# Agent attention and a rational feed-forward layer on one core: every second product with v written to the upper half of the partitions

## The chip, the cores and the metric

The kernel runs on one core of a Trainium2 chip. The metric is device microseconds of one execution. Each time comes from repeated executions; a profile is one further execution with the hardware profiler on. TensorE multiplies matrices into PSUM, VectorE, ScalarE and GpSimd work elementwise, and SyncE (SP) issues the transfers.

## The reference

Two batches of 12480 tokens with 128 channels go through attention over 49 "agents" and then through a feed-forward layer with a rational activation of 2048 hidden units:

```
def sm(a, b):
    s = scale * (a @ b.transpose(0, 2, 1))
    s = s - s.max(-1, keepdims=True)
    e = np.exp(s)
    return e / (e.sum(-1, keepdims=True) + 1e-09)
a2k = sm(agents, k)              # 49 x 12480 for each batch
agent_v = a2k @ v                # 49 x 128
q2a = sm(q, agents)              # 12480 x 49
attn_out = q2a @ agent_v
h = x @ w_in                     # x: attn_out as (24960, 128)
P = a[0] + a[1] * h + a[2] * h2 + a[3] * h3
Q = 1.0 + np.abs(b[0]) * np.abs(h) + np.abs(b[1]) * h2
return (P / (Q + 1e-06)) @ w_out
```

The change is in `a2k @ v`: the sum over 12480 keys (padded to 98 chunks of 128) of a 49 x 128 product. A column of ones beside v gives the sum of the exponentials with it, so a product has 129 columns.

## The kernel before

**Two stages.** The first stage (up to about 66 us) does all of the attention of batch 0: scores of agents and keys (`sc_wide`, L209), their maxima (`mx_pe1`, `mx_pe2`, L227 and L235, which VectorE reads in L230 and L238), the exponentials (`ex_sub` L243, `ex_exp` L247) and the products with v (`pv_pe`, L253). Beside them the weights, which come in as 64-bit words, are decoded to float32 (`decode`: ScalarE L171 and L172, VectorE L175 to L178, GpSimd L181 and L182, VectorE L185). The second stage is the main loop (`main`) over 278 units of three chunks each: `mm1` (L439, L440) makes hidden values in one of two PSUM slots, ScalarE (L501, L515, L517), VectorE (L522, L530, L535) and GpSimd (L568, L573) the rational function, and `mm2` (L447) multiplies by w_out some units later. Every engine executes its instructions in the order in which the program issues them.

**Products of batch 0.** The 98 chunks are ten groups of 10 (`G0`); the last has 8. A chunk's exponentials, 128 keys by 49 agents, are the stationary operand, its part of v the moving one. Groups 0 to 4 add up in PSUM bank 4, groups 5 to 9 in bank 5, since the two have different maxima. After group 5 (`HG`) VectorE takes bank 4 times the factor `fac` (L783), at the end it adds bank 5 (L786), and `av_norm` (L263 to L265), the transpose (`avt_pe`, L268, to L271 and L272) and four matmuls with w_in (`m_pe`, L275) follow, which the main loop needs. Decoding of weight blocks stands between the groups in VectorE's order (`DECS`: behind groups 1, 3, 5 and 7). The queries' first scores (L374) stand behind group 2, their transposes (L401) behind group 7. At the end four products of the identity with itself (L789) run on TensorE.

**Products of batch 1.** They are 25 groups of up to 4 chunks (`G1`) in `a2k_stream`, of which the main loop takes one step per unit, when the PSUM bank that the output doesn't use is free: TensorE's part of the step runs behind `mm2`, the evictions one unit later (`pv_ev`, L257 for the first, L259 for others). Each group is a sum of its own in PSUM; VectorE adds them up in `av_acc`. `q_stream` takes steps beside it with the same bank.

Of the kernel before, what the change touches and what calls it, by code (L numbers as in the profile page):

```python
# [11 lines left out]
F32 = mybir.dt.float32  # L12
# [4 lines left out]
ALU = mybir.AluOpType  # L17
# [4 lines left out]
C = 128  # L22
A = 49
# [8 lines left out]
KR = 113  # L32
LO = 64
# [30 lines left out]
HG, MX1, MX2 = 5, 5, 0  # L64
# [16 lines left out]
def agent_attention_rational_moe(  # L81
# [12 lines left out]
    PE, ACT, DVE, POOL, SP = nc.tensor, nc.scalar, nc.vector, nc.gpsimd, nc.sync  # L94

    const = ctx.enter_context(tc.tile_pool(name="const", bufs=1))
# [5 lines left out]
    outs = [ps_p.tile([128, 512], F32, name=f"outb{i}") for i in range(2)]  # L102

    ident = const.tile([128, 128], F32, name="ident")
# [10 lines left out]
    S = const.tile([CK, NCK, A], F32, name="S")  # L115
    mx = const.tile([CK, 4, A], F32, name="mx")
    mb = const.tile([CK, 2, A], F32, name="mb")
    m49 = const.tile([A, 2], F32, name="m49")
    av_acc = const.tile([A, C + 1], F32, name="av_acc")
    avt = const.tile([128, KR], F32, name="avt")  # L120
    m_hi = [const.tile([128, DFF], F32R, name=f"m_hi{b}") for b in range(B)]
    m_lo = [const.tile([128, DFF], F32R, name=f"m_lo{b}") for b in range(B)]
# [6 lines left out]
    def ring(pool, n, shape, dt, nm):  # L129

        r = rings.setdefault((pool.name, nm), [[], 0])
        if len(r[0]) < n:
            r[0].append(pool.tile(shape, dt, name=f"{nm}_{len(r[0])}"))
        r[1] += 1
        return r[0][(r[1] - 1) % n]
# [4 lines left out]
    def load_k(pool, b, G, g, bufs):  # L140
        n = min(G, NCK - g * G) * CK
        t = ring(pool, bufs, [128, G * CK], F32, f"k{b}")
        o = b * NKP + g * G * CK
        for i in ((0, n // 2), (n // 2, n)) if (b, g) == (0, 0) else ((0, n),):
            SP.dma_start(out=t[:, i[0]:i[1]], in_=kT[:, o + i[0]:o + i[1]])
        k_t[b, g] = t

    def load_v(pool, b, G, g, bufs):
        n = min(G, NCK - g * G)
        t = ring(pool, bufs, [CK, G * (C + 1)], F32, f"v{b}")  # L150
        o = g * G * (C + 1)
        SP.dma_start(out=t[:, :n * (C + 1)], in_=vP[b, :, o:o + n * (C + 1)])
        v_t[b, g] = t.rearrange("p (c d) -> p c d", d=C + 1)
# [65 lines left out]
    def sc_pe(b, G, g, bank):  # L219
        kt = k_t.pop((b, g))  # L220
        for c in range(min(G, NCK - g * G)):
            PE.matmul(bank[:CK, c * A:(c + 1) * A], lhsT=kt[:, c * CK:(c + 1) * CK], rhs=ag[:, b * A:(b + 1) * A], start=True, stop=True)  # L222
# [3 lines left out]
    def mx_pe1(bank, src):  # L226
        PE.transpose(bank[:A, :CK], src, ident[:CK, :CK])  # L227

    def mx_ev1(bank, k=0):
        DVE.tensor_reduce(out=m49[:, k:k + 1], in_=bank[:A, :CK], axis=AX.X, op=ALU.max)  # L230
        st["d"] = ring(sm_p, 1, [A, A], F32, "d49")
        DVE.tensor_scalar(out=st["d"], in0=ident[:A, :A], scalar1=m49[:, k:k + 1], scalar2=None, op0=ALU.mult)
# [13 lines left out]
        s = S[:, g * G:min(g * G + G, NCK), :]  # L246
        ACT.activation(out=s, in_=s, func=AF.Exp, scale=SCALE)  # L247

    def pv_pe(b, G, g, bank, first, last):
        vt = v_t.pop((b, g))  # L250
        n = min(G, NCK - g * G)
        for c in range(n):
            PE.matmul(bank[:A, :C + 1], lhsT=S[:, g * G + c, :], rhs=vt[:, c, :], start=first and c == 0, stop=last and c == n - 1)  # L253

    def pv_ev(first, bank):
        if first:
            DVE.tensor_copy(out=av_acc, in_=bank[:A, :C + 1])  # L257
        else:
            DVE.tensor_tensor(out=av_acc, in0=bank[:A, :C + 1], in1=av_acc, op=ALU.add)  # L259

    def av_norm(src):
        r = ring(sm_p, 1, [A, 1], F32, "avr")
        DVE.tensor_scalar(out=r, in0=src[:, C:C + 1], scalar1=EPS, scalar2=None, op0=ALU.add)  # L263
        DVE.reciprocal(out=r, in_=r)
        DVE.tensor_scalar(out=av_acc[:, :C], in0=src[:, :C], scalar1=r, scalar2=co["rho_s"][:A], op0=ALU.mult, op1=ALU.mult)  # L265
# [360 lines left out]
    def a2k_stream(kv, b, G):  # L626
        ng = -(-NCK // G)
        load_k(kv, b, G, 0, 2)
        load_k(kv, b, G, 1, 2)
        yield (None, None, [])  # L630
        yield (None, None, [])
        for g in range(ng):
            if 1 <= g < ng - 1:
                load_k(kv, b, G, g + 1, 2)
            if g >= ng - 2:
                load_v(kv, b, G, g + 2 - ng, 2)

            def cp(bk, g=g):
                n = min(G, NCK - g * G)
                ACT.copy(out=S[:, g * G:g * G + n, :], in_=bk[:CK, :n * A].rearrange("p (c a) -> p c a", a=A))  # L640

            yield (None, lambda bk: sc_pe(b, G, g, bk), [("ACT", cp), ("DVE", lambda bk, g=g: group_max(G, g, bk))])
        row = 3 * ((ng - 2) // 2 % 2 == 0)
        yield (None, lambda bk: mx_pe1(bk, mx[:, row, :]), [("DVE", lambda bk: mx_ev1(bk))])
        yield (None, lambda bk: mx_pe2(bk), [("DVE", lambda bk: mx_ev2(bk))])
        for g in range(-2, ng):
            evs = []
            if g + 2 < ng:
                evs.append(("POOL", lambda bk, g=g: ex_sub(G, g + 2, POOL)))
            if 0 <= g + 1 < ng:  # L650
                evs.append(("ACT", lambda bk, g=g: ex_exp(G, g + 1)))
            if g < 0:
                yield (None, None, evs)
                continue
            if 1 <= g < ng - 1:
                load_v(kv, b, G, g + 1, 2)
            evs.append(("DVE", lambda bk, g=g: pv_ev(g == 0, bk)))
            yield (None, lambda bk: pv_pe(b, G, g, bk, True, True), evs)
        yield (None, None, [("DVE", lambda bk: av_norm(av_acc))])
        yield (None, avt_pe, [("DVE", avt_ev)])  # L660
        for pc in range(4):
            yield (None, lambda bk: m_pe(pc, bk), [("ACT", lambda bk: m_rnd(b, pc, bk)), ("DVE", lambda bk: m_rest(b, pc, bk))])

    with tc.manual_schedule():
        nc.scalar.preload_act_table_set("natural_log_exp_and_others")
        G = G0
        ng = -(-NCK // G)
        with tc.tile_pool(name="st", bufs=1) as sp, tc.tile_pool(name="pst", bufs=1, space=bass.MemoryType.PSUM) as pp:
            bank = [pp.tile([128, 512], F32, name=f"bank{i}") for i in range(6)]
# [23 lines left out]
            def load_next(g, most=99):  # L693

                while most > 0 and wanted and ready(*wanted[0], g):
                    kind, h = wanted.pop(0)
                    most -= 1
                    if kind == "v":
                        load_v(sp, 0, G, h, VB)
                    elif kind == "q":  # L700
                        load_q(h)
                    else:
                        raws[kind, h] = ring(sp, 4, [128, WP, 2], I32, "raw")
                        load_w(raws[kind, h], {"i": w_in, "o": w_out}[kind], h)
# [20 lines left out]
            for g in range(ng):  # L725
                bk = (bank[2 * (g % 3)], bank[2 * (g % 3) + 1])
# [26 lines left out]
                ex_sub(G, e, DVE)  # L753
                ex_exp(G, e)
            for g in range(ng):
                pv_pe(0, G, g, bank[4 if g < HG else 5], g in (0, HG), g in (HG - 1, ng - 1))
                if g == QPE:
                    q_pe(0, bank[0])
                    q_ev(0, bank[0])
                    q_exp(0)  # L760
                    q_sum(0)
                    for f in q_split(0):
                        f()
                if g == MX2:
                    mx_pe1(outs[0], mx[:, 1, :])
                    mx_ev1(outs[0], 1)
                if g == MX2 + 1:
                    mx_pe2(outs[1], 1)
                    mx_ev2(outs[1], 1)
                    for e in range(HG, ng):  # L770
                        ex_sub(G, e, DVE if e < HG + SUB_DVE else POOL, 1)
                        ex_exp(G, e)
                    fac = ring(sm_p, 1, [A, 1], F32, "fac")
                    DVE.tensor_tensor(out=fac, in0=m49[:, 0:1], in1=m49[:, 1:2], op=ALU.subtract)
                    ACT.activation(out=fac, in_=fac, func=AF.Exp, scale=SCALE)
                dec_at(g)
                if g == QTR:
                    q_tr(0, 0, bank[1])
                    q_tr(0, 1, bank[3])
                    q_trev(0, 0, bank[1], ACT.copy)  # L780
                    q_trev(0, 1, bank[3], ACT.copy)
                if g == HG:
                    DVE.tensor_scalar(out=av_acc, in0=bank[4][:A, :C + 1], scalar1=fac, scalar2=None, op0=ALU.mult)  # L783
                load_next(g)
            assert not wanted and not decs
            DVE.tensor_tensor(out=av_acc, in0=bank[5][:A, :C + 1], in1=av_acc, op=ALU.add)  # L786
            av_norm(av_acc)
            for _ in range(DUA):
                PE.matmul(outs[0][:, :128], lhsT=ident, rhs=ident, start=True, stop=True)  # L789
# [64 lines left out]
```

## Time and profile before

| | |
|---|---|
| median of 3 runs | 1321.06 us (1320.81 to 1327.85) |
| profiled execution | 1321.58 us |
| its span, first to last instruction | 1319.7 us |
| TensorE busy | 1255.2 us (95%) |
| VectorE busy | 1196.1 us (91%) |
| ScalarE busy | 1166.5 us (88%) |
| GpSimd busy | 1153.7 us (87%) |
| mean granted TensorE clock | 0.992 |

The busy shares are averages over both stages. In the rows below PE is TensorE's matmul, PEld its weight load, DVE VectorE, ACT ScalarE, POOL GpSimd, SPq the queue of SyncE. Matmuls overlap, and the end of one is modelled, so the start of one record against that of the next says more than its duration. [...]

### The profile page before, as it was taken

How to read it: one execution, taken by the hardware profiler on the slowest of the kernel's cores; microseconds unless marked ns; L12 is line 12 of the kernel's file. 1: busy time of each engine (PE TensorE's matmuls, PEld its weight loads, DVE VectorE, ACT ScalarE, POOL GpSimd, SP SyncE). 2: the span in 40 equal slices, each digit the busy share in tenths (PEclk: the TensorE clock that was granted, in tenths of full speed). 3: DMA queues.
4: the chain of work that ended last, by engine and by line, in shares of the span. 5: the costliest groups of instructions: out<-in, count | busy, mean ns of one | idle time of the engine just before them, and what ended most of it. 6: DMA issues, size and time to landing. Idle time of an engine off the chain costs nothing.

```text
span 1319.7 us, 13309 instructions
## 1 busy us (share of the span) xinstructions
PE 1255.2 (95%) x4815; PEld 786.3 (60%) x4815; DVE 1196.1 (91%) x984; ACT 1166.5 (88%) x736; POOL 1153.7 (87%) x562
## 2 busy tenths in 40 slices
PE   8979999998999999998999999999999999999998
PEld 8756666665566566665555555655655555565553
DVE  5888999989988888988999999999999999999996
ACT  3468999998889898997999999999999999999995
POOL 3448988988999998988899999999999999999991
PEclk9989999999999999999999999999999999999999
DMA  9411111111011111100000000000000000000000
GB/s 367 184 48 47 40 55 46 40 59 38 22 57 47 41 53 48 39 27 23 16 23 30 23 15 23 23 15 23 30 23 15 23 23 31 8 30 8 16 7 26
DMA packets 22971, 56.55 MB, mean 43 GB/s; under 512 B 2800, under 2 KB 9712, under 8 KB 22896
## 3 DMA queue, kind: packets, MB, share of 16 engines
q1 hardware_dynamic: 22896, 55.61, 12.7%
q8 instruction: 40, 0.66, 0.2%
q14 instruction: 35, 0.29, 0.1%
HBM read 42.82 MB, written 12.78 MB: 42 GB/s over the span
## 4 chain that ended last, share of the span: by engine, by line
PE 47%; DVE 23%; ACT 13%; POOL 9%; issue 6%; DMA 1%; SPq 0%; DVEq 0%; POOLq 0%; ACTq 0%
PE outb L447 25%; DVE u L522 8%; DVE w L530 8%; PE slot L439 8%; PE slot L440 7%; ACT x L501 6%; POOL u L568 5%; ACT w L517 3%; POOL u L573 3%; PE outb L374 3%; ACT w L515 2%; DVE u L535 2%; PE outb L253 2%; PE bank L209 1%; PE outb L222 1%
## 5 line engine op out<-in xcount | busy, mean ns | idle before, releaser
L447 PE MATMUL outb<-u,wo 128*128 128x480 f32 x1664 | 726.2, 571 | 36.6 <-DVE pT L406 21.4
L568 POOL TENSOR_TENSOR u<-u,w 128x1440 f32<-128x1440 f32 x204 | 668.6, 3290 | 0.0
L530 DVE SCALAR_TENSOR_TENSOR w<-slot,cf,x 128x1440 f32<-128x1440 f32 x278 | 474.9, 1708 | 89.8 <-ACT x L501 85.0
L447 PEld LDWEIGHTS outb<-u,wo 128*128 128x128 f32 x1664 | 309.5, 189 | 314.3 <-issue 230.5
L501 ACT ACTIVATE x<-slot,cf 128x1440 f32<-128x1440 f32 x278 | 405.5, 1459 | 96.7 <-PE slot L440 68.4
L522 DVE SCALAR_TENSOR_TENSOR u<-x,cf,slot 128x1440 f32<-128x1440 f32 x278 | 472.6, 1700 | 0.0
L573 POOL TENSOR_SCALAR u<-u,cf 128x1440 f32<-128x1440 f32 x204 | 387.8, 1902 | 93.7 <-DVE u L522 72.5
L439 PE MATMUL slot<-pT,m_hi 113*128 113x480 f32 x832 | 375.6, 452 | 10.9 <-DVE u L522 10.5
L515 ACT ACTIVATE w<-w,cf 128x2880 f32<-128x2880 f32 (+1 forms) x140 | 374.6, 2676 | 0.0
L517 ACT ACTIVATE w<-w 128x2880 f32<-128x2880 f32 (+1 forms) x140 | 361.8, 2585 | 0.0
L440 PE MATMUL slot<-pT,m_lo 113*128 113x480 f32 x832 | 317.4, 382 | 0.0
L439 PEld LDWEIGHTS slot<-pT,m_hi 113*128 113x128 f32 x832 | 157.6, 189 | 82.8 <-DVE u L522 40.9
L440 PEld LDWEIGHTS slot<-pT,m_lo 113*128 113x128 f32 x832 | 157.9, 190 | 40.8 <-issue 23.4
L535 DVE SCALAR_TENSOR_TENSOR u<-u,cf,w 128x1440 f32<-128x1440 f32 x74 | 134.0, 1816 | 0.0
L374 PEld LDWEIGHTS outb<-ag,q 128*120 128x120 f32 x400 | 45.6, 185 | 12.7 <-issue 8.2
L374 PE MATMUL outb<-ag,q 128*120 128x49 f32 x400 | 44.9, 265 | 0.9 <-DVE pT L406 0.7
L401 PEld LDWEIGHTS outb<-ident,p 120*113 120x113 f32 x200 | 27.5, 177 | 23.2 <-issue 20.0
L222 PEld LDWEIGHTS outb<-ag,k 128*128 128x128 f32 x196 | 26.4, 197 | 15.7 <-issue 8.8
L406 DVE CAST pT<-outb 113x480 fp32r<-113x480 f32 x50 | 32.4, 648 | 0.0
L454 ACT COPY o<-outb 128x480 f32<-128x480 f32 x42 | 23.0, 547 | 9.2 <-PE outb L447 9.2
L253 PEld LDWEIGHTS outb<-v,S 128*49 128x49 f32 x196 | 20.3, 123 | 17.6 <-issue 12.0
L401 PE MATMUL outb<-ident,p 120*113 120x120 f32 x200 | 29.2, 267 | 0.0
(132 smaller groups left out, 504.3 us busy)
## 6 DMA issues: line engine op xcount, KB each, us to landing
q<-qT SPq DMA_DIRECT2D x26, 480.0 KB, 3.4
outT<-o SPq DMA_DIRECT2D x52, 240.0 KB, 2.0
v<-vP SPq DMA_DIRECT2D x24, 258.0 KB, 2.7
k<-kT SPq DMA_DIRECT2D x24, 256.0 KB, 2.6
v<-vP SPq DMA_DIRECT2D x9, 645.0 KB, 11.1
k<-kT SPq DMA_DIRECT2D x8, 640.0 KB, 8.9
raw<-w_in SPq DMA_DIRECT2D x4, 512.0 KB, 10.8
raw<-w_out SPq DMA_DIRECT2D x2, 512.0 KB, 10.6
```

The source lines that it names most:

```text
L374: PE.matmul(bank[:CH, c * A:(c + 1) * A], lhsT=qt[:, c * CH:(c + 1) * CH], rhs=ag[:, b * A:(b + 1) * A], start=True, stop=True)
L439: PE.matmul(s[:, j, :BT], lhsT=m_hi[b][:KR, f], rhs=rhs, start=True, stop=False)
L440: PE.matmul(s[:, j, :BT], lhsT=m_lo[b][:KR, f], rhs=rhs, start=False, stop=True)
L447: PE.matmul(outs[blk % 2][:, :BT], lhsT=wo[:, fc, :], rhs=g[:, j, :], start=fc == 0, stop=fc == NFC - 1)
L501: ACT.activation(out=x, in_=h, func=AF.Square, bias=co["xb"])
L515: ACT.activation(out=r, in_=r, func=AF.Ln, bias=arm["lb"])
L517: ACT.activation(out=r, in_=r, func=AF.Exp, scale=-1.0)
L522: DVE.scalar_tensor_tensor(out=y, in0=x, scalar=co["kap"], in1=h, op0=ALU.add, op1=ALU.mult)
L530: DVE.scalar_tensor_tensor(out=w, in0=h, scalar=co["mu"], in1=x, op0=ALU.max, op1=ALU.add)
L535: DVE.scalar_tensor_tensor(out=view("u", u), in0=view("u", u), scalar=arm["om"], in1=view("w", u), op0=ALU.add, op1=ALU.mult)
L568: POOL.tensor_tensor(out=view("u", g), in0=view("u", g), in1=view("w", g), op=ALU.mult)
L573: POOL.tensor_scalar(out=y, in0=y, scalar1=1.0, scalar2=arm["om"], op0=ALU.mult, op1=ALU.add)
```

## The change

In both batches the even chunks of a group write PSUM partitions 0 to 48 and the odd ones 64 to 112 (`LO` = 64, `KR` = 113). The two halves must be added. [...] Batch 0 does this twice, once for bank 4 (the copy behind group 5, the matmul behind group 6) and once for bank 5; batch 1 adds up both halves at once over all groups (113 partitions instead of 49) and does it once at the end, in a step of its own.

```
+    av_two = const.tile([KR, C + 1], F32, name="av_two")
-    def pv_pe(b, G, g, bank, first, last):
+    def pv2_pe(b, G, g, bank, first=True, last=True):
         vt = v_t.pop((b, g))
         n = min(G, NCK - g * G)
         for c in range(n):
-            PE.matmul(bank[:A, :C + 1], lhsT=S[:, g * G + c, :], rhs=vt[:, c, :], start=first and c == 0, stop=last and c == n - 1)
+            o = c % 2 * LO
+            PE.matmul(bank[o:o + A, :C + 1], lhsT=S[:, g * G + c, :], rhs=vt[:, c, :], start=first and c < 2, stop=last and c >= n - 2)
-    def pv_ev(first, bank):
+    def pv2_ev(first, bank):
         if first:
-            DVE.tensor_copy(out=av_acc, in_=bank[:A, :C + 1])
+            DVE.tensor_copy(out=av_two, in_=bank[:KR, :C + 1])
         else:
-            DVE.tensor_tensor(out=av_acc, in0=bank[:A, :C + 1], in1=av_acc, op=ALU.add)
+            DVE.tensor_tensor(out=av_two, in0=bank[:KR, :C + 1], in1=av_two, op=ALU.add)
+    def pv2_sum(bank):
+        PE.matmul(bank[:A, :C + 1], lhsT=ident[LO:KR, LO:KR], rhs=av_two[LO:KR, :], start=True, stop=True)
+    def pv2_both(bank):
+        DVE.tensor_tensor(out=av_acc, in0=bank[:A, :C + 1], in1=av_two[:A, :], op=ALU.add)
+        av_norm(av_acc)
...
-        yield (None, None, [("DVE", lambda bk: av_norm(av_acc))])
+        yield (None, pv2_sum, [("DVE", pv2_both)])
...
-                pv_pe(0, G, g, bank[4 if g < HG else 5], g in (0, HG), g in (HG - 1, ng - 1))
+                pv2_pe(0, G, g, bank[4 if g < HG else 5], g in (0, HG), g in (HG - 1, ng - 1))
+                if g == HG + 1:
+                    pv2_sum(outs[0])
...
                 if g == HG:
+                    DVE.tensor_copy(out=av_two[LO:KR, :], in_=bank[4][LO:KR, :C + 1])
                     DVE.tensor_scalar(out=av_acc, in0=bank[4][:A, :C + 1], scalar1=fac, scalar2=None, op0=ALU.mult)
+                if g == HG + 1:
+                    DVE.scalar_tensor_tensor(out=av_acc, in0=outs[0][:A, :C + 1], scalar=fac, in1=av_acc, op0=ALU.mult, op1=ALU.add)
...
+            DVE.tensor_copy(out=av_two[LO:KR, :], in_=bank[5][LO:KR, :C + 1])
+            pv2_sum(outs[1])
             DVE.tensor_tensor(out=av_acc, in0=bank[5][:A, :C + 1], in1=av_acc, op=ALU.add)
+            DVE.tensor_tensor(out=av_acc, in0=outs[1][:A, :C + 1], in1=av_acc, op=ALU.add)
             av_norm(av_acc)
```

## Rows read from the trace of the kernel before

**Rows 1.** Busy time in stretches of the span; columns as in the first line.

```profile
core 0: us, PE busy (x) PEld busy (x) DVE busy (x) ACT busy (x) POOL busy (x), PEclk, DMA share, GB/s
30.00:58.00 28.00, 26.46 (x231) 25.12 (x229) 25.08 (x44) 11.93 (x23) 13.90 (x12) 1.00 0.58 224
...
355.00:590.00 235.00, 232.03 (x920) 144.22 (x920) 205.88 (x167) 212.81 (x139) 216.51 (x114) 1.00 0.16 46
700.00:1200.00 500.00, 476.78 (x1666) 286.45 (x1665) 472.23 (x336) 471.16 (x261) 477.50 (x210) 1.00 0.07 22
```

**Rows 2.** The same stretches, for ScalarE's first instruction of a unit (L501) alone.

```profile
355.00:590.00 235.00, 73.10 (x50) 1.00 0.16 46
700.00:1200.00 500.00, 171.12 (x117) 1.00 0.07 22
```

**Rows 3.** The chain of waits from 355 to 590 us, shares by line.

```profile
by line: PE outb L447 38.9%; PE slot L439 13.1%; PE slot L440 11.1%; PE outb L253 8.9%; DVE w L530 5.8%; DVE u L522 5.5%; ACT x L501 5.0%; PE outb L374 2.8%; issue 1.9%; DVE u L535 1.7%; ACT w L517 1.1%; ACT w L515 1.1%; PE outb L401 1.0%; 
```

**Rows 4.** Timeline of TensorE's matmuls around one group of batch 1; start, duration.

```profile
429.28 1.77 PE L447 MATMUL outb<-u,wo 128*128 128x480 f32 x4
430.98 1.09 PE L253 MATMUL outb<-v,S 128*49 128x129 f32 x8
432.00 0.49 PE L439 MATMUL slot<-pT,m_hi 113*128 113x480 f32 x1
```

**Rows 5.** Timeline of TensorE's matmuls in the first stage.

```profile
33.92 2.41 PE L253 MATMUL bank<-v,S 128*49 128x129 f32 x20
36.27 0.42 PE L235 MATMUL outb<-d,ones 49*128 49x49 f32 x2
...
38.96 1.88 PE L374 MATMUL bank<-ag,q 128*120 128x49 f32 x16
40.77 11.27 PE L253 MATMUL bank<-v,S 128*49 128x129 f32 x100
51.97 1.08 PE L401 MATMUL bank<-ident,p 120*113 120x120 f32 x8
52.98 4.19 PE L253 MATMUL bank<-v,S 128*49 128x129 f32 x36
```

**Rows 6.** Timeline of VectorE in the first stage, with its idle time before.

```profile
35.59 0.24 DVE L232 TENSOR_SCALAR d<-ident,m 49x49 f32<-49x49 f32 x1
36.73 0.21 DVE L238 COPY mb<-outb 128x49 f32<-128x49 f32 x1 [0.89 <-PE outb L235]
...
53.29 0.34 DVE L783 TENSOR_SCALAR av_acc<-bank,fac 49x129 f32<-49x129 f32 x1
...
57.91 0.28 DVE L786 TENSOR_TENSOR av_acc<-bank,av_acc 49x129 f32<-49x129 f32 x1
```

**Rows 7.** Timeline of TensorE's weight loads around the group of rows 4.

```profile
430.98 0.17 PEld L253 LDWEIGHTS outb<-v,S 128*49 128x49 f32 x2 [0.70 <-ACT x L501]
...
431.68 0.12 PEld L253 LDWEIGHTS outb<-v,S 128*49 128x49 f32 x1
...
432.00 0.19 PEld L439 LDWEIGHTS slot<-pT,m_hi 113*128 113x128 f32 x1 [0.19 <-issue]
...
433.20 0.41 PEld L447 LDWEIGHTS outb<-u,wo 128*128 128x128 f32 x2
```

**Rows 8.** The instructions of tile av_acc: duration least, median, most in ns.

```profile
L257 DVE COPY av_acc<-outb x1: 278/278/278, 357.7 to 357.7; 49x129 f32<-49x129 f32 x1
```

**Rows 9.** Busy time in the two stretches of half clock (PEclk 0.50).

```profile
60.80:64.20 3.40, 3.40 (x6) 1.27 (x5) 1.34 (x3) 1.37 (x2) 1.53 (x2) 0.50 0.42 113
...
91.50:98.30 6.80, 6.80 (x18) 4.99 (x19) 4.86 (x5) 2.87 (x4) 5.62 (x6) 0.50 0.14 39
```

**Rows 10.** Timeline from the last sum to the loop's first ScalarE instruction.

```profile
59.26 0.26 PE L268 MATMUL bank<-ident,av_acc 49*128 49x49 f32 x1 [1.00 <-DVE av_acc L265]
59.56 0.20 ACT L271 COPY avt<-bank 128x49 f32<-128x49 f32 x1 [3.98 <-PE bank L268]
60.15 3.09 PE L275 MATMUL outb<-wi,avt 128*113 128x512 f32 x4 [0.63 <-DVE avt L272]
...
66.90 1.47 ACT L501 ACTIVATE x<-slot,cf 128x1440 f32<-128x1440 f32 x1 [0.67 <-DMA k<-kT]
```

**Rows 11.** Waits of SP's own queue from 25 to 66 us: total, times, longest.

```profile
SPq L164 <- DVE wo L185: 16.5, 1, 16.5
```

More of the change, by code (lines that the diff above doesn't have):

```diff
@@ L656, in a2k_stream @@
                 load_v(kv, b, G, g + 1, 2)
-            evs.append(("DVE", lambda bk, g=g: pv_ev(g == 0, bk)))
-            yield (None, lambda bk: pv_pe(b, G, g, bk, True, True), evs)
-        yield (None, None, [("DVE", lambda bk: av_norm(av_acc))])
+            evs.append(("DVE", lambda bk, g=g: pv2_ev(g == 0, bk)))
+            yield (None, lambda bk: pv2_pe(b, G, g, bk), evs)
+        yield (None, pv2_sum, [("DVE", pv2_both)])
         yield (None, avt_pe, [("DVE", avt_ev)])
```

## The prediction

> **What bounds the kernel now.** I read the page first: its share of busy time (TensorE 95%, VectorE 91%, ScalarE 88%, GpSimd 87%) names no bound, because the kernel has two stages that both hold the changed products. So the second view is the table of stretches. In 30 to 58 us TensorE is busy 26.46 of 28.00 us and VectorE 25.08; in 355 to 590 us, where the products of batch 1 run inside the main loop, TensorE is busy 232.03 of 235.00 us and GpSimd 216.51; in 700 to 1200 us, without them, every engine lies near 95% [rows 1]. The reader is to see that only in the second stretch one engine stands out. The third view counts units of the loop by their first ScalarE instruction: 50 in 235 us are 4.70 us each, 117 in 500 us are 4.27 [rows 2]. So the loop is slower where batch 1 is worked on, and TensorE is why. The fourth view, the chain of waits of that stretch, says how much of it is L253: 8.9% of 235 us, 20.9 us [rows 3]. There are 25 groups of products in it (98 products, four to a group), each some 1.02 us from its first record to the next line's [rows 4], together some 25; so about 83% of what is taken from a group should come off the time.
>
> In the first stage I put the timeline of TensorE [rows 5] beside that of VectorE [rows 6]. TensorE ends its last product of batch 0 at about 57.1 us. VectorE comes to the last sum, L786, at 57.91 us, straight from decoding weights and not from a wait. So VectorE sets that end, with TensorE 0.8 us behind its back: a gain on TensorE alone is worth little here.
>
> **The products, part by part.** A product in float32 is two records: 196 records are 98 products. A run of 100 records takes 11.27 us with the last one's latency of 0.27 in it (20 records in 2.41 and 36 in 4.19 give 0.113 and 0.112), so one takes (11.27 - 0.27)/99 = 0.111 us [rows 5]. The change sends every second product to the other half of the partitions. If the two halves work at the same time, but records start in order and a product's second record follows its first on the same half, then the second record of one product runs with the first of the next. Eight records take five steps and not eight, twenty take eleven. Nothing in the trace has a matmul on partitions 64 and up alone, so it can't show this. The bounds are: no gain (eight steps), and three steps of 0.111 = 0.33 us a group.
>
> What the trace shows is near this. Entering and leaving a group costs a pause: L447 ends streaming at 429.28 + 4 x 0.40 = 430.88 us and the first load of L253 is at 430.98; the group ends streaming at about 431.90 and the load of L439 stands at 432.00, whereas the load of L447 at 433.20 is made while L440 still streams [rows 4, 7]. So a stationary block of 49 columns is already treated as another shape, and alternation between two such blocks doesn't add a shape. I take it that the halves overlap. [...]
>
> [...] First the row: the loads of L253 go on at the pace of the matmuls, the second 0.05 us behind the first (two are 0.17 us, one 0.12) [rows 7], and 0.111 a record leaves no room for an uncovered load. [...] The row stands for one half only, so the uncovered load is a rival below.
>
> **Main loop.** 24 groups x 0.33 and 0.11 of the last, short one are 8.1 us of TensorE; 83% of it is 6.7 us. The added sum with the identity is one group more: two records and two pauses, 0.22 + 0.20 = 0.4 us, paid on the same chain. VectorE's added instruction is priced by the copy, 0.28 us [rows 8]; VectorE is idle 29 us of this stretch, which hides it; without cover it costs its 0.28. The wider evictions (113 partitions for 49) read the same 129 elements each, so I price them at nothing: lower bound zero, upper bound doubled, 25 x 0.28 = 7 us of an engine with 29 us free. Sum: -6.3 us. Check against other engines: 235 - 6.3 = 228.7 us makes GpSimd 94.7% busy, VectorE 90.0%, ScalarE 93.1%, all under the 95.5%, 94.4% and 94.2% that they reach in 700 to 1200 us [rows 1]. So no other engine stops the gain.
>
> **First stage.** Here order matters. The sum of the upper half of bank 4 is issued on TensorE behind group 6 and needs VectorE's copy of that half, which stands just ahead of L783, behind the decoding of a weight block. Behind this sum on TensorE wait group 7, the transposes of q, groups 8 and 9.
>
> - VectorE gets a little earlier: mb (L238) waits 0.89 us for L235, which is queued behind group 1. With group 1 at eleven steps, it ends at 35.2 us; L232 is done at 35.83, L235 starts at about 35.9 and not 36.27, so 0.4 us are gained [rows 5, 6]. L783's place comes at 52.9, the copy there ends at 53.2.
> - TensorE gets far ahead: L235 until 36.2, group 2 until 37.5, q until 39.3, groups 3 to 6 (41 steps, 4.6 us) until 43.9. It then stands idle until 53.2 us: 9.3 us. Before, it reached this place at 40.77 + 80 x 0.111 = 49.6.
> - From 53.2 it still has: the sum 0.4, group 7 1.2, transposes with their pauses 1.0, a pause 0.1, groups 8 and 9 (19 steps) 2.1: 4.8 us at 2.4 GHz. But it comes out of a pause. The granted clock was at 0.50 (1.2 GHz) from 60.8 to 64.2 us, after a stretch with pauses of 1.0 and 0.6, and from 91.5 to 98.3 [rows 9, 10]. A pause of 9 us should bring it there too; one such stretch costs half its length, 1.7 to 3.4 us. I take 1.7, that of the nearest row. TensorE ends at 59.7, its result stands at 60.0 to 60.2.
> - VectorE's own work: copy 0.28, L783, a wait of some 0.3 for the sum, one instruction like L783 (0.34), and the decoding of 4.28 (53.63 to 57.91): it is there at 58.6, before TensorE. So TensorE is late next.
> - Tail: copy 0.28 (60.48), the sum by the pattern of L268 to L271 (0.30 and the issue: 60.85), with L786 under its cover, one more add 0.28: 61.1. L786 ended at 58.19. The stage loses 2.9 us; 1.2 if the clock stays at 2.4 GHz, 4.6 with the longer stretch.
>
> This delay isn't hidden later: av_acc, L268, the four L275 and the first slot follow each other up to the loop's first ScalarE instruction at 66.90 us [rows 10]. The queue of SP stood 16.5 us at its next load of weights, for VectorE's L185 [rows 11], which is shifted likewise, so these loads move along with their users.
>
> Sum: -6.3 + 2.9 = -3.4 us. The profiled execution took 1321.58 us (span 1319.7, 1.9 around it), 0.5 above the median of 1321.06: 1318.2 us.
>
> **Rivals.**
> 1. Loads uncovered (chance 0.20). At each change of half a load of about 0.043 us shows (0.17 less 0.12), then a product costs 0.111 + 0.043 = 0.154: a group saves 0.2 us. Main loop: 24 x 0.2 x 0.83 - 0.3 = -3.8; first stage 1.1 more for the 28 products left, +4.0. 1321.8 us.
> 2. No overlap at all (0.14), the other side: products go one after another as before. The wait for the copy then decides alone. TensorE is at the sum at 49.6, waits until 53.6, has 0.4 + 2.2 + 1.0 + 0.1 + 4.0 = 7.7 us left, and ends at 61.3, or 63.0 with a slow stretch; with the tail the stage loses 4.2 to 5.9 us, the loop another 0.3: 1326 to 1328 us. It decides as soon as a group of eight takes over 0.8 us.
> 3. A pause at each change of half (0.05): 0.10 us more, on rival 2, for each of 98 products in the loop (83% of 9.8 us) and of the 28 behind the first sum (2.8 us): 1327 + 8 + 3 = 1338. Against it speaks that both blocks have the same 49 columns.
> 4. Both slow stretches of the clock go (0.13). TensorE was busy all of the 3.4 and 6.8 us at half clock [rows 9]; at 2.4 GHz they give back up to 1.7 and 3.4 us. The denser work just ahead of L275 speaks for the first, nothing for the second but that it is moved: 1318.2 - 5.1 = 1313.1.
>
> **How the numbers follow.** My forecast has the rest, 0.48, with a range of its own of 1315.5 to 1321. No change that can be told is within 0.5%, 6.6 us: 1314.5 to 1327.7. Faster: rival 4, with a little of the forecast's edge, 0.14. Slower: rival 3 and the upper part of rival 2, 0.14. The range leaves out rival 3 and the edges of 2 and 4: 1313 to 1327.5.
>
> **What would show it.** Right: in the main loop a group of eight L253 records (now another line) takes 0.6 and not 1.0 us, and 355 to 590 us hold one to two units more; in the first stage TensorE idles 9 us ahead of the sum with a granted clock of 0.5 behind it, and the first ScalarE instruction of the loop comes at about 70 us. Wrong: groups of 0.9 us (rival 2), of 0.7 (rival 1), the loop's start at 67 us or earlier (the stall is hidden, or TensorE isn't that far ahead), or a loop that keeps 4.70 us a unit though its groups are shorter: then TensorE wasn't its bound.

## The result, and the profile after

In the first comparison the changed kernel took 1314.54 us in the median of 7 runs (1313.03 to 1318.83), the kernel before 1327.85 (7 runs, 1320.81 to 1330.11): ratio 0.9915, 95% interval 0.9888 to 0.9942 (the two medians alone would give 0.990, as that of the kernel before lies among its longer times). The forecast was 1318.2 us in a range of 1313.0 to 1327.5. The times of most kernels here lie in two groups 6 to 9 us apart, for a reason shown below (one instruction near the end); a second comparison, with 12 runs of the change, gave 0.9963 (0.9935 to 0.9990). So the change is faster, by 0.4% to 0.85% according to how many runs of each kernel fell into which group; both intervals lie below 1. The two profiled executions, 1321.58 and 1315.57 us, both belong to the shorter times (that instruction takes 3.06 us in each); their 6.0 us are taken apart here.

The starts of the units' first ScalarE instruction, read from the two timelines, say where the time went:

| | before | after | gained in the stretch |
|---|---|---|---|
| unit 0 (end of the first stage) | 66.90 | 70.42 | -3.52 |
| unit 60 | 344.02 | 346.94 | 0.60 |
| unit 112 (products of batch 1 over) | 585.97 | 583.39 | 5.50 |
| unit 130 | 670.81 | 664.89 | 3.34 |
| unit 277 (last) | 1295.30 | 1289.32 | 0.06 |

**A group of products.** The timeline of TensorE after, around one group of batch 1, which answers to [rows 4]:

```profile
420.50 2.58 PE L457 MATMUL outb<-u,wo 128*128 128x480 f32 x6
423.01 0.65 PE L256 MATMUL outb<-v,S 128*49 128x129 f32 x8
423.58 0.48 PE L449 MATMUL slot<-pT,m_hi 113*128 113x480 f32 x1
```

Cut to the start of the group, the same timeline shows loads and matmuls in pairs:

```profile
423.00 0.13 PEld L256 LDWEIGHTS outb<-v,S 128*49 128x49 f32 x2 [0.70 <-ACT x L511]
423.01 0.32 PE L256 MATMUL outb<-v,S 128*49 128x129 f32 x2
```

Eight records take 0.65 us with the last one's duration of 0.27 in it, where they took 1.09. The reader is to see that two records stand within 0.32 us: one of them alone takes 0.312 us, so the second starts about 0.01 us behind the first. The others follow in pairs too, at 423.15, 423.26 and 423.38 us: eight records are four pairs, four steps. From its first record to the next line a group takes 0.57 us and not 1.02: 0.44 us less, where 0.33 was forecast. The pauses on entering and leaving are near those of before, 0.09 and 0.08 us against 0.10: L457's last record starts at 422.51 and streams for 0.40, like those ahead of it, and the first load stands at 423.00; the last pair streams until 423.38 + 0.11 = 423.49, and L449 starts at 423.58.

**The stretch of the products**, unit 60 to unit 112, in the table of stretches; columns as in [rows 1]. Before:

```profile
344.02:585.97 241.95, 238.18 (x937) 147.23 (x936) 213.43 (x172) 219.51 (x145) 222.92 (x116) 1.00 0.15 46
```

After:

```profile
346.94:583.39 236.45, 228.06 (x937) 136.28 (x936) 214.63 (x172) 219.05 (x144) 223.45 (x117) 1.00 0.16 47
```

TensorE's busy time fell by 238.18 - 228.06 = 10.1 us, the stretch by 5.5: the rest turned into idle time of TensorE (3.8 us before, 8.4 after). The chain of waits after, in the same stretch, answers to [rows 3], which has it from 355 to 590 us of the kernel before:

```profile
by line: PE outb L457 22.1%; DVE u L532 11.1%; issue 9.9%; ACT x L511 9.4%; PE slot L449 8.6%; DVE w L540 8.2%; PE slot L450 7.4%; ACT w L525 5.3%; PE outb L384 3.6%; DVE u L545 3.3%; ACT w L527 3.3%; PE outb L256 2.8%; DVE pT L416 1.3%; DV
```

The share of L447 (now L457) falls from 38.9% to 22.1%, and that of all TensorE lines shown from 75.8% to 44.5%; VectorE's and ScalarE's lines take their place. GpSimd stands in neither row as shown.

**The first stage.** TensorE after, answering to [rows 5], and VectorE, answering to [rows 6]:

```profile
43.55 6.12 PE L256 MATMUL bank<-v,S 128*49 128x129 f32 x80
55.11 0.66 PE L265 MATMUL outb<-av_two,ident 49*49 49x129 f32 x2 [5.45 <-DVE av_two L795]
55.71 2.39 PE L256 MATMUL bank<-v,S 128*49 128x129 f32 x20
58.03 1.95 PE L411 MATMUL bank<-ident,p 120*113 120x120 f32 x8
59.91 2.38 PE L256 MATMUL bank<-v,S 128*49 128x129 f32 x36
62.69 0.42 PE L265 MATMUL outb<-av_two,ident 49*49 49x129 f32 x2 [0.40 <-DVE av_two L801]
```

```profile
54.76 0.30 DVE L795 COPY av_two<-bank 49x129 f32<-49x129 f32 x1
...
55.82 0.34 DVE L798 SCALAR_TENSOR_TENSOR av_acc<-outb,fac,av_acc 49x129 f32<-49x129 f32 x1 [0.38 <-PE outb L265]
...
58.88 0.68 DVE L186 SCALAR_TENSOR_TENSOR wo<-z,r 128x512 f32<-128x512 f32 x1
62.33 0.30 DVE L801 COPY av_two<-bank 49x129 f32<-49x129 f32 x1 [2.77 <-PE bank L256]
...
63.46 0.15 DVE L273 TENSOR_SCALAR avr<-av_acc 49x1 f32<-49x1 f32 x1
```

TensorE waits 5.45 us for the copy of bank 4's upper half to `av_two`, which the matmul with the identity reads, and then VectorE waits 2.77 us for TensorE. The granted clock, in the table of stretches after, answers to [rows 9]:

```profile
36.50:46.60 10.10, 9.48 (x70) 8.72 (x70) 8.51 (x21) 6.61 (x13) 3.08 (x3) 0.50 0.74 274
53.50:60.30 6.80, 5.19 (x34) 4.23 (x36) 5.52 (x11) 2.08 (x4) 4.79 (x3) 0.50 0.00 0
65.10:68.40 3.30, 3.29 (x7) 1.24 (x8) 1.77 (x3) 1.78 (x3) 0.69 (x1) 1.00 0.44 96
```

Twenty records take 2.39 us behind the pause of 5.45 us, at a granted clock of 0.50, and 1.31 at 1.00 (below). The third row is the four matmuls with w_in: at 1.00 now, while before they met the 0.50 of [rows 9]. The first row is a stretch that the kernel before doesn't have. It follows a pause that grew with the shorter products of group 0, before and after:

```profile
33.68 0.31 PE L227 MATMUL outb<-ident,mx 128*49 128x128 f32 x1 [1.54 <-DVE mx L191]
```

```profile
35.06 0.31 PE L228 MATMUL outb<-ident,mx 128*49 128x128 f32 x1 [2.65 <-DVE mx L192]
```

All seven profiles with the changed first stage have this pause of 2.65 us and a stretch at half clock that begins at 34.1 to 36.7 us; none of the seven with the first stage of before has one there.

And 1.37 us of the later start have nothing to do with the change: the first transfers of k landed later in this execution, as they did, by 1.1 and 0.5 us, in two profiles with the first stage of before (the loop's change and the step alone, below). TensorE's first run of scores in each, before and after:

```profile
8.62 11.41 PE L209 MATMUL bank<-ag,k 128*128 128x98 f32 x100 [0.73 <-DMA k<-kT]
```

```profile
9.99 11.41 PE L210 MATMUL bank<-ag,k 128*128 128x98 f32 x100 [2.15 <-DMA k<-kT]
```

From the copy's place (L783 before) to the normalisation (L263, now L273) it is 4.94 us before and 8.70 after, from there to the loop's first ScalarE instruction 8.67 and 6.96.

**The end of batch 1.** The 3.34 us between units 112 and 130 come from one place, unit 114 to 115: 9.44 us before, 5.54 after; the other units of the stretch give 0.56 of these 3.90 back. The timeline before, of GpSimd, VectorE and TensorE there:

```profile
590.82 3.30 POOL L568 TENSOR_TENSOR u<-u,w 128x1440 f32<-128x1440 f32 x1
591.72 2.48 DVE L265 TENSOR_SCALAR av_acc<-av_acc,avr,cf 49x128 f32<-49x128 f32 x1
...
599.00 0.64 DVE L406 CAST pT<-outb 113x480 fp32r<-113x480 f32 x1
599.70 1.60 PE L447 MATMUL outb<-u,wo 128*128 128x480 f32 x2 [3.65 <-DVE pT L406]
```

and after:

```profile
594.82 1.07 PE L457 MATMUL outb<-u,wo 128*128 128x480 f32 x2 [1.61 <-DVE pT L416]
...
602.67 0.90 DVE L275 TENSOR_SCALAR av_acc<-av_acc,avr,cf 49x128 f32<-49x128 f32 x1
```

Before, the last step of the normalisation runs beside a product of GpSimd, takes 2.48 us and ends 0.08 us behind it (594.20 and 594.12 us), and it stands ahead of the second transpose of q (L406), for which TensorE then waits 3.65 us, where the loop goes over to the next block of 480 queries. After, the step for the sum of the halves lies between, the normalisation comes three units later, and TensorE waits 1.61 us.

### The profile page after: what moved, and what is told of

It reads as the page before. It is cut to its first block, busy times and chain, and to the rows that moved or that the text cites. A ratio compares the mean times of both kernels' runs of the same rounds, so it can differ in the third digit from the quotient of the medians.

```text
span 1313.7 us, 13330 instructions
## 1 busy us (share of the span) xinstructions
PE 1238.9 (94%) x4821; PEld 768.8 (59%) x4821; DVE 1196.2 (91%) x989; ACT 1166.7 (89%) x736; POOL 1154.7 (88%) x562
## 4 chain that ended last, share of the span: by engine, by line
PE 43%; DVE 24%; ACT 15%; POOL 9%; issue 8%; DMA 1%; SPq 0%; DVEq 0%; POOLq 0%; ACTq 0%
PE outb L457 22%; DVE u L532 9%; DVE w L540 9%; ACT x L511 7%; PE slot L449 7%; PE slot L450 6%; POOL u L578 5%; ACT w L527 3%; ACT w L525 3%; POOL u L583 3%; PE outb L384 3%; DVE u L545 2%; PE bank L210 1%; PE outb L223 1%; DVE pT L416 1%
## 5 line engine op out<-in xcount | busy, mean ns | idle before, releaser
L457 PE MATMUL outb<-u,wo 128*128 128x480 f32 x1664 | 725.7, 570 | 36.6 <-DVE pT L416 19.7
L457 PEld LDWEIGHTS outb<-u,wo 128*128 128x128 f32 x1664 | 309.2, 189 | 314.0 <-issue 230.5
L449 PE MATMUL slot<-pT,m_hi 113*128 113x480 f32 x832 | 374.3, 450 | 11.0 <-DVE u L532 10.6
L449 PEld LDWEIGHTS slot<-pT,m_hi 113*128 113x128 f32 x832 | 157.0, 189 | 82.9 <-DVE u L532 41.0
L545 DVE SCALAR_TENSOR_TENSOR u<-u,cf,w 128x1440 f32<-128x1440 f32 x74 | 135.3, 1834 | 0.0
L223 PE MATMUL outb<-ag,k 128*128 128x49 f32 x196 | 25.4, 274 | 3.8 <-DVE mx L201 3.7
```

The lines of the kernel that those rows point to most:

```text
L449: PE.matmul(s[:, j, :BT], lhsT=m_hi[b][:KR, f], rhs=rhs, start=True, stop=False)
L457: PE.matmul(outs[blk % 2][:, :BT], lhsT=wo[:, fc, :], rhs=g[:, j, :], start=fc == 0, stop=fc == NFC - 1)
L545: DVE.scalar_tensor_tensor(out=view("u", u), in0=view("u", u), scalar=arm["om"], in1=view("w", u), op0=ALU.add, op1=ALU.mult)
```

## The experiments

**The loop's change alone**: the first stage is that of before.

```
-                pv2_pe(0, G, g, bank[4 if g < HG else 5], g in (0, HG), g in (HG - 1, ng - 1))
-                if g == HG + 1:
-                    pv2_sum(outs[0])
+                pv_pe(0, G, g, bank[4 if g < HG else 5], g in (0, HG), g in (HG - 1, ng - 1))
...
```

> Only batch 1 (the main loop) has the change; the first stage is that of before. Theory (the first stage loses 2.2 us to the wait on TensorE, the loop gains by itself): the loop's first ScalarE instruction at 66.9 us, or 1.4 later where a transfer of k lands late, then the same loop as with the whole change: about 2 us less than with it, some 9 us less than before. Rival (the first stage costs nothing, its later start is a late transfer alone): the same time as with the whole change, 6 us less than before.

1313.38 us against 1321.95 of before, ratio 0.9941 (0.9919 to 0.9964); unit 0 at 66.54 us though k came 1.1 us late. Units 60 to 112 take 236.37 us, as with the whole change. The theory holds: the loop gains by itself, and the first stage gives part of it back. (That unit 0 comes even earlier than expected is the clock at the four matmuls with w_in, at 1.00 in this profile: the first four records take 1.94 us there, and 3.09 before.)

**The first stage's change alone.**

```
-            evs.append(("DVE", lambda bk, g=g: pv2_ev(g == 0, bk)))
-            yield (None, lambda bk: pv2_pe(b, G, g, bk), evs)
-        yield (None, pv2_sum, [("DVE", pv2_both)])
+            evs.append(("DVE", lambda bk, g=g: pv_ev(g == 0, bk)))
+            yield (None, lambda bk: pv_pe(b, G, g, bk, True, True), evs)
+        yield (None, None, [("DVE", lambda bk: av_norm(av_acc))])
```

> Only batch 0 (the first stage) has the change; the loop is that of before. Theory: TensorE waits some 5 us ahead of the sum of bank 4, works at 1.2 GHz behind it and ends behind VectorE; the loop starts 2.2 us later than before for equal arrival of k, and the time is 2 us more than before. Rival (no cost): equal to before within 0.5 us.

1324.11 us against 1321.95, ratio 1.0012 (0.9988 to 1.0036): by the time alone no cost can be told. By the trace it can. From the copy's place to the normalisation it takes 9.30 us against 4.94, to unit 0 16.26 against 13.61. The theory holds by the trace, with a cost above the 2.2 us that it named: counted from the first run of scores behind the transfer of k, unit 0 comes 3.2 us later than before.

**The added step alone**, without any overlap:

```
+        yield (None, None, [])
         yield (None, None, [("DVE", lambda bk: av_norm(av_acc))])
```

> The kernel before with one empty step ahead of the last normalisation of batch 1, and no overlap anywhere. Theory (4 us of the gain come from where the added step puts this normalisation, away from the change of block): the interval from unit 114 to 115, 9.4 us before, falls to about 5.5 us, and the time to about 1317.5. Rival (these 4 us come from the shorter products): the interval stays near 9.4 us and the time at that of before.

The interval of units 114 to 115 is 5.81 us against 9.44. On VectorE's timeline the instruction that took 2.48 us is short:

```profile
596.67 0.56 DVE L265 TENSOR_SCALAR av_acc<-av_acc,avr,cf 49x128 f32<-49x128 f32 x1
```

1317.11 us in the median, ratio 0.9977 (0.9952 to 1.0002): as forecast, but the time alone isn't clear of noise. Units 60 to 112 take 241.97 us, as before. By the interval of the units the theory holds: an empty step, which computes nothing, gives 3.6 of these 3.9 us. It moves the normalisation away from GpSimd's product and behind the second transpose at once; how much is due to which isn't shown.

**Even chunks first, then odd ones**, in batch 1:

```
-        for c in range(n):
+        for c in range(n) if b == 0 else [*range(0, n, 2), *range(1, n, 2)]:
```

> The whole change, but in batch 1 a group's even chunks are issued first and the odd ones behind them. Theory (records start in order, so halves overlap only where neighbours lie on different halves): seven steps for eight records, a group of 0.88 us from its first record to the next line and not 0.7, and some 3 us more than with the whole change. Rival (the queue lets a record of the free half pass one that waits): groups as short as with the whole change, and the same time.

TensorE's timeline around a group:

```profile
423.23 0.66 PE L256 MATMUL outb<-v,S 128*49 128x129 f32 x8
423.81 0.48 PE L449 MATMUL slot<-pT,m_hi 113*128 113x480 f32 x1
```

and cut to the start of the group:

```profile
423.23 0.33 PE L256 MATMUL outb<-v,S 128*49 128x129 f32 x2
```

The group takes 0.58 us to the next line, as with the whole change (0.57), and units 60 to 112 236.90 us. Two records start within 0.02 us here too, though the first four in order of issue are all of one half, where records follow each other at 0.111 us. The rival holds, and my rule of the order falls: by these starts, records of the free half overtake waiting ones of the other. So what I wrote of the kernel before, that every engine executes in the order of issue, as TensorE and VectorE do in [rows 5, 6], doesn't hold for these matmuls on two halves. The time, 1322.55 us in the median with 0.9982 (0.9959 to 1.0005), is higher for another reason: 8 of its 10 runs lie among the longer times, and the profiled one of them met the long instruction near the end (9.48 us, below); the other two took 1314.09 and 1315.15 us, as the whole change does.

**Half of the products left out.**

```
-        for c in range(n):
+        for c in range(n - n // 2) if n == 4 else range(n):
```

> The loop's change alone, with two of the four products of each group of batch 1 left out (half of the sum over keys is missing). A group takes some 0.36 us on TensorE and not 0.58, 5 us less over the stretch. Theory (half of what the overlap saved was lost because other engines are near their limit there; past this point little comes through): units 60 to 112 take at most 1.5 us less than with the loop's change alone. Rival (TensorE is still the bound of the stretch): at least 2.5 us less, the same half of what is saved.

Busy time from unit 60 to 112 (columns as above):

```profile
343.41:578.31 234.90, 223.34 (x841) 130.99 (x840) 215.44 (x172) 218.69 (x145) 224.02 (x117) 1.00 0.16 47
```

TensorE is 4.7 us less busy than with the loop's change alone (228.06), the stretch 1.5 us shorter (236.37): a third comes through, just inside what the theory allowed.

**GpSimd's subtraction left out.**

```
-            if g + 2 < ng:
-                evs.append(("POOL", lambda bk, g=g: ex_sub(G, g + 2, POOL)))
```

> The loop's change alone, without GpSimd's subtraction of the maxima in batch 1 (the exponentials are taken of the scores as they are). That is 23 to 25 instructions, some 17 us of GpSimd, in the stretch of the products. Theory (behind the shorter products GpSimd, at 94% there, is what holds the loop): units 60 to 112 take at least 3 us less than the 236.4 us of the loop's change alone. Rival (no single engine holds it, each is waited for in turn): at most 1.5 us less.

```profile
345.60:580.13 234.53, 227.72 (x937) 136.38 (x936) 212.69 (x172) 218.81 (x145) 210.67 (x94) 1.00 0.16 47
```

GpSimd is 12.7 us less busy than with the loop's change alone (223.35), the units 60 to 112 take 1.8 us less (234.53): between what the two expected, nearer to the rival. GpSimd isn't what holds the loop, and by the run before it TensorE alone isn't either, behind the shorter products. Whether VectorE or ScalarE alone does was not tested.

**The sum of bank 4 behind all products.**

```
-                if g == HG + 1:
-                    pv2_sum(outs[0])
...
+            pv2_sum(outs[0])
+            DVE.scalar_tensor_tensor(out=av_acc, in0=outs[0][:A, :C + 1], scalar=fac, in1=av_acc, op0=ALU.mult, op1=ALU.add)
             DVE.tensor_copy(out=av_two[LO:KR, :], in_=bank[5][LO:KR, :C + 1])
             pv2_sum(outs[1])
```

> The whole change, but the sum of bank 4's upper half is issued behind the last product of batch 0, with that of bank 5; VectorE's use of it moves there too. Theory (the first stage's loss is TensorE's wait in the middle and the slow clock behind it): TensorE runs through groups 7 to 9, VectorE alone sets the end, with four instructions of 0.3 us more than before; from the resumption of the scores behind the late transfer of k to the loop's first ScalarE instruction 59 us or less, where the whole change took 60.4 to 61.5. Rival (the loss is VectorE's added instructions in the tail, wherever the sum stands): 60.4 or more.

It took 62.7 us. Of these, 1.6 come from a stretch at half clock in the scores, from 11.3 to 14.7 us (100 records took 13.04 us there and not 11.41); the 61.1 that are left lie on the rival's side as well. The parts bear out something of each: from the copy's place to the normalisation it takes 6.24 us against 8.70, so the wait in the middle did cost 2.5 us, and VectorE's added instructions, with what they wait for, 1.3 (6.24 - 4.94). But TensorE, done early, idles 4.45 us ahead of the last sum, and the granted clock is 0.50 from 59.0 to 69.2 us, where it now matters most, in the four matmuls with w_in (3.73 us for the first four records, where they take 1.94 at 1.00):

```profile
61.55 0.66 PE L265 MATMUL outb<-av_two,ident 49*49 49x129 f32 x2 [4.45 <-DVE av_two L799]
```

```profile
59.00:69.20 10.20, 7.03 (x16) 3.91 (x17) 5.33 (x14) 1.21 (x3) 4.20 (x4) 0.50 0.21 53
```

From the normalisation to unit 0 it takes 9.67 us against 6.96: the 2.5 us are lost again. 1315.93 us in the median, ratio 0.9953 (0.9929 to 0.9976).

**The clock held with 20, then 36 products of the identity.**

```
                 if g == HG + 1:
+                    for _ in range(20):
+                        PE.matmul(outs[0][:, :128], lhsT=ident, rhs=ident, start=True, stop=True)
                     pv2_sum(outs[0])
```

> The whole change with 20 products of the identity with itself on TensorE ahead of the sum of bank 4, into a bank that the sum overwrites. They fill the wait of 5.5 us with some 4.5 us. Theory (about half of the loss is the clock at 1.2 GHz behind the wait): granted clock 1.00 from 55 us on, products of batch 0 over about 2.5 us earlier than 62.3, and the loop's start 1.5 to 3 us earlier than with the whole change. Rival (TensorE's clock doesn't matter, VectorE sets the end): loop's start unchanged within 0.5 us.

> As the run with 20 products of the identity ahead of the sum of bank 4, whose filling ended at 51.7 us and left 4.2 us of pause, in which the clock fell all the same; now 36, some 8 us of work for a pause of 8.9. Theory (about half of the first stage's loss is the clock at 1.2 GHz behind the pause): granted clock 1.00 from 54 to 61 us, the products of batch 0 over at 51.6 us after the resumption of the scores and not 53.4, and the loop's start about 1.8 us earlier than in the run with 20. Rival (VectorE sets the end): at most 0.5 us earlier.

With 20 nothing was tested: the filling ended at 51.7 us, 4.17 us ahead of the sum, and the clock stood at 0.50 from 53.8 to 60.6. With 36 it stood at 1.00 from 46.1 to 62.0:

```profile
57.25 0.42 PE L265 MATMUL outb<-av_two,ident 49*49 49x129 f32 x2
57.60 1.31 PE L256 MATMUL bank<-v,S 128*49 128x129 f32 x20
...
62.43 0.42 PE L265 MATMUL outb<-av_two,ident 49*49 49x129 f32 x2 [0.39 <-DVE av_two L803]
```

From the one sum to the other it takes 5.2 us there, 7.6 with the whole change and 8.2 to 8.3 in three other profiles in which this part is the same: the clock costs 2.4 to 3.1 us behind the pause. But now the filling is too long: the sum starts 2.7 us behind its copy. From the resumption of the scores to the loop's start it takes 60.7 us, against 61.7 in the run with 20, which would be 1.0 us gained. The first run of scores in each, with 20 and with 36, speaks against that:

```profile
9.28 13.04 PE L210 MATMUL bank<-ag,k 128*128 128x98 f32 x100 [1.48 <-DMA k<-kT]
```

```profile
9.49 11.41 PE L210 MATMUL bank<-ag,k 128*128 128x98 f32 x100 [2.02 <-DMA k<-kT]
```

The run with 20 met half clock in its scores and lost 1.6 us there. Counted from the end of these scores the loop starts 48.7 us later with 20 and 49.3 with 36; two profiles of the whole change have 49.0 and 50.1. So the theory holds for the clock's price, and no gain at the loop's start is shown, as the rival expected. The medians are 1315.11 us, 0.9944 (0.9911 to 0.9976), with 20; 1320.46 us, 0.9969 (0.9945 to 0.9993), with 36.

**One unit's product on GpSimd, near the end.** The profile of the loop's change alone has an interval of 13.1 us between units 275 and 276, where the kernel before has 5.1. Its timeline, of VectorE, GpSimd and TensorE:

```profile
1272.90 9.48 DVE L557 SCALAR_TENSOR_TENSOR u<-u,cf,w 128x1440 f32<-128x1440 f32 x1
...
1267.96 12.91 POOL L590 TENSOR_TENSOR u<-u,w 128x1440 f32<-128x1440 f32 x4
...
1282.44 5.13 PE L469 MATMUL outb<-u,wo 128*128 128x480 f32 x6 [7.14 <-DVE u L557]
```

The same instruction in the profile of before:

```profile
1283.43 3.06 DVE L535 SCALAR_TENSOR_TENSOR u<-u,cf,w 128x1440 f32<-128x1440 f32 x1
```

The median of its line there is 1.71 us. In the profile of the loop's change alone GpSimd executes four products in a row, from 1267.96 to 1280.87, and VectorE's, which starts in the second, ends 1.5 us behind the fourth. In the kernel before it starts in the second as well and gets in between two of them: it ends at 1286.49, 1.5 us behind the second (1284.97), and the third takes 4.68 us, where the median is 3.28. In four other profiles with longer times it took 6.28 us once and about 9.5 three times, in the other six with shorter times about 3.1. The change was to give this unit's product to GpSimd:

```
-        return u % ON_DVE != ON_DVE - 1 and u < NU - LAST_DVE
+        return (u % ON_DVE != ON_DVE - 1 or u == 267) and u < NU - LAST_DVE
```

(with its addition of a constant as well).

> The loop's change alone, and the last product of unit 267 with w goes to GpSimd and not to VectorE, as for its neighbours. Theory (the times over 1317 of every kernel here come from this one instruction of VectorE near the end, which takes 3.1 or 9.5 us where its like take 1.7, while GpSimd works through four products in a row): no interval of over 6 us between two units behind unit 270, and all times in 1309 to 1314 us. Rival (the long instruction is a symptom, something else stops the loop there): some times remain 6 to 9 us above the rest.

> The loop's change alone with unit 267 on GpSimd, again, beside the whole change. Theory (no long instruction of VectorE near the end): all times in 1309 to 1314 us. Rival: some above 1317 us.

> The whole change, unaltered, beside the others on the same chip. Theory (VectorE's long instruction near the end is met or missed by chance in every kernel that has it): besides times of 1313 to 1317 us some 6 to 9 us above, as in a third of the runs of the kernel before. Rival (the whole change avoids it): none above 1319.

All 12 runs of this version, six in each of two sets, took 1310.18 to 1313.26 us: ratios 0.9916 (0.9888 to 0.9945) and 0.9912 (0.9883 to 0.9941). The interval of units 275 to 276 is 3.93 us, and VectorE's next such instruction is short:

```profile
1287.80 1.72 DVE L557 SCALAR_TENSOR_TENSOR u<-u,cf,w 128x1440 f32<-128x1440 f32 x1
```

The whole change, beside it, took 1314.41 to 1316.28 us in six runs and 1321.92 to 1323.29 in six (median 1319.10, 0.9963, 0.9935 to 0.9990). The theory holds for both: the long instruction is what parts the two groups, and the whole change doesn't avoid it. It, with 1311.45 us in the second set, is the best of the kernels here that leave nothing out.

## Why the prediction was right, and where it was not

The direction and the range held, and the two large terms had the right sign: -6.7 forecast for the loop's shorter groups, -5.5 measured from unit 60 to 112; +2.9 for the first stage, +3.52 measured. Their nearness is in part luck. The 3.52 are 3.76 from the copy's place to the normalisation, 1.37 of a late transfer and 0.10 ahead of the copy, less 1.71 behind the normalisation, most of it the clock that the four matmuls with w_in met. And the sum in the profiled executions was -6.0 where I had -3.4: the loop gave 1.2 less, the first stage took 0.6 more, units 0 to 60 gave 0.6 that I had not forecast, and the added step gave 3.3 where I had a cost of 0.4. My 0.72 for "within 0.5%" was right for one of two comparisons, 0.37%, and not for the other, 0.85%. What failed is inside the sum.

- **"Records start in order ... eight records take five steps."** That the two halves overlap at all I had taken without a run that showed it; the pairs show it. Eight records take four steps; a group saves 0.44 us and not 0.33, 10.1 us of TensorE over the stretch and not 8.1. The run with even chunks first showed that the order of issue doesn't decide it.
- **"83% of what is taken from a group should come off the time."** 5.5 of 10.1 us came off, 54%. The share of L253 in the chain says how often it stands there now, not how long the next chain is. My check with the other engines' busy shares found room, and there was none for all of it: halving the products again brought a third of what they saved, and freeing GpSimd of 12.7 us brought 1.8. This error and the one before it partly cancelled.
- **The added step.** I priced its matmul and its VectorE instruction, and not what it moves: the normalisation, away from GpSimd's product and from the place where the next queries are waited for. That is 3.3 us, the largest part that I had not seen; the empty step alone gave 3.6.
- **The first stage.** The mechanism was right: TensorE runs ahead, waits for the copy (5.45 us, 9.3 forecast, since the granted clock was at 0.50 through group 2 and the scores of q, 36.5 to 46.6 us, behind a pause that the shorter group 0 had lengthened and that I had not seen coming), restarts at a granted clock of 0.50 and ends behind VectorE. From the copy's place to the normalisation I had 4.94 + 3.3; it was 4.94 + 3.8 here and 4.94 + 4.4 and 4.5 in three other profiles with this part unchanged. The term that was too small is the clock: 1.7 us taken, 2.4 to 3.1 measured. No run shows the 2.4 and 1.2 GHz of the prediction and the expectations: the traces have the granted clock as a share, 1.00 and 0.50, at which twenty records of the products took 1.31 and 2.39 us. Ahead of the copy I had a gain of 0.4 us; L235 met the half clock, so 0.1 was gained behind it, and the copy's place, counted from the resumption of the scores, came 0.1 us later than before.
- **Rival 4** was half right: the four matmuls with w_in met the full clock, and from the normalisation to unit 0 it took 1.7 us less; the second slow stretch stayed (0.50 from 94.5 to 101.3 us). The first isn't shown to be the change's merit: of the seven profiles with the first stage of before, five met the full clock there too (7.22 us from normalisation to unit 0) and two didn't (8.67), the profile of before among them. Against those five the changed first stage costs 3.5 to 4.2 us from the copy's place to unit 0, and not the 2.1 that the two profiles compared here show.
- **Rivals 1 to 3** are refuted by the group's 0.57 us and by the pairs 0.01 us apart, of matmuls and of loads: two loads stand within 0.13 us, one of which takes 0.12 by itself, though both halves use all 128 rows. The two halves gave 1.8 times (1.02 to 0.57 us, pauses included).

What it would bring to hold the clock in the first stage with a filling of the right length stays open, and so does which chain holds units 60 to 112 now; the runs only show that neither TensorE nor GpSimd alone does.

## What to carry to other kernels

Where a stationary block is as narrow as the 49 columns here, writing to two PSUM halves can shorten TensorE's work (1.8 times here), but only the stage in which TensorE set the time gained, and there only a part: the loop kept 5.5 of 10.1 us, and the first stage, where VectorE set the end, lost 2 to 4 us through a sum in the middle that made TensorE wait for VectorE (5.45 us) and come back at a granted clock of 0.50. Price what a new step moves, not only what it computes. And before times that differ by half a percent are compared, look for an instruction whose duration differs between profiles of kernels that are alike in it.

## What the runs showed of the hardware that was not expected

- Products that write the two halves of the partitions started independently of the order of issue: 0.579 us a group by turns, 0.586 with all even chunks first, both from the starts of the records, against 1.018 on one half.
- VectorE's product of u and w (L535, L545, L557), both in SBUF, took 3.06, 6.28 or 9.48 us near the end, where the median of its line is 1.71, while GpSimd executed products of u and w that followed each other without a gap. In the two profiles set out above it started in the second of them; it ended 1.5 us behind the end of that one (3.06 us) and 1.5 us behind that of the fourth (9.48 us). The 6.28 us lie 3.2 us from each of the others, about a product of GpSimd (median 3.28). VectorE's L522 and L530, which read a PSUM slot, took 1.72 us at the most in the profile of before.
- With the whole pause of TensorE filled, the granted clock stood at 1.00 behind it (46.1 to 62.0 us, one profile); with a filling of 4.7 us and 4.2 us left open it stood at 0.50 (53.8 to 60.6 us).
